# Attention and a mixture of experts in one kernel: attention order, routing, slot lists and slot tiles rewritten

## The chip, the cores and the metric

The kernel runs on one core of a Trainium2 chip. The metric is the device time of one execution in microseconds (us). The engines are named as in the profile: PE (TensorE, with PEld for its weight loads), DVE (VectorE), ACT (ScalarE), POOL (GpSimd) and SP (SyncE, which here only issues DMAs). Each engine takes its instructions strictly in the order in which they are queued; an instruction that waits holds up those behind it.

## The reference

Eight sequences of 448 tokens with 12 heads of 64 values go through attention with normalised queries and keys. The 3584 rows of 768 values that come out go through one dense block and one of eight experts, chosen by the largest logit.

```python
def _attn_ref(q, k, v, g_q, g_k):            # 8 x 12 x 448 x 64
    q_n, k_n = rmsnorm(q, g_q), rmsnorm(k, g_k)
    scores = scale * np.matmul(q_n, k_n.transpose(0, 1, 3, 2))
    ...                                       # softmax over the keys
    return np.matmul(attn, v)
x = attn_out.transpose(0, 2, 1, 3).reshape(3584, 768)
y_dense = np.maximum(x @ w1_dense, 0.0) @ w2_dense      # 768 -> 512 -> 768
expert_idx = np.argmax(x @ w_gate, axis=1)              # 8 experts
gate_w = softmax(x @ w_gate)[expert_idx]
y_moe[mask] = gate_w[mask, None] * (np.maximum(x[mask] @ w1[e], 0.0) @ w2[e])
return y_dense + y_moe
```

## The kernel before

*Attention.* Two heads side by side are a pair, and two pairs a group `g`; there are 24 groups, three to a sequence `b`. A token's row is split as position p and j = 0..6, so that seven consecutive tokens lie in one partition and a partition's load is one run of 1792 bytes. `period(g)` is one turn of a software pipeline, an order written out by hand over i = 0..6: it issues the scores of group g+1 (`scores`, four products of 64x64 tiles for each j, then ACT's exponential into one of 14 buffers), the value products of group g (`attend`, 64 rows each, a pair of them on the two halves of the array), the division (`divide`), the transposes of the group two before (`xtrans`, `xturned`), normalising and turning of q and k of group g+2 (`normalise`, `transposes`, `turned`), squares, sums and norms of group g+3 (`squares` on POOL, `sums` on DVE, `norms` on ACT), and the loads of group g+5 on SP. v comes through POOL's queue, cast to bf16 on the way. One pool of four PSUM banks (`wk`) serves transposes, value products, dense block, logits and ranks; the tile that `norms` writes its result to is the tile that `xtrans` fills next.

*Dense block and routing.* `dense` runs the first dense product for a chunk of 128 tokens as filler between attention steps, four chunks a sequence of which the last overlaps the one before by 64 rows. `logits`, `choose`, `gates`, `ranks` and `places` find for each token its expert, its gate and its slot: tiles of 128 slots are given to experts in the order in which they fill. `scatter` writes a record per token (its row, its dense hidden row, gate and number, 2592 bytes) to its slot in a table in HBM.

*Slot tiles.* `listing` orders the tiles that are full after six sequences, `experts` and `gaps` finish the list and mark empty slots. `turn(t)` reads a tile's number from the list (`tei`) into a register of SP, loads gates and numbers, and loads the 128 records with a DMA transpose. `gemm1(t)` multiplies by the expert's first matrix (chosen by a register of PE, six products of 512 columns), ACT applies the relu and the gate, `htrans(t)` turns the hidden rows (four transposes), and `gemm2(t)` sums dense and expert product in one PSUM tile, which DVE copies out and an indirect DMA of POOL writes to the output. `tiles` keeps four loads ahead. 32 tiles run always; three more stand behind a branch at the end.

Of the kernel before, what the change touches and what calls it, by code (L numbers as in the profile page):

```python
# [18 lines left out]
def kernel(  # L19
# [28 lines left out]
    De = D + 1  # L48
    scale = 1.0 / (D ** 0.5)
    PE, DVE, ACT, POOL, SP = (mybir.EngineType.PE, mybir.EngineType.DVE,  # L50
# [8 lines left out]
    nc.scalar.preload_act_table_set("natural_log_exp_and_others")  # L59
    make_identity(nc, ident)  # L60
    eps_t = const.tile([P, 1], F32)
    nc.vector.memset(eps_t, 1e-6)
    gq2 = const.tile([P, 1], F32)
    gk2 = const.tile([P, 1], F32)
    for hh in range(2):
        nc.scalar.dma_start(gq2[hh * D:(hh + 1) * D, :], g_q.unsqueeze(1))
        nc.scalar.dma_start(gk2[hh * D:(hh + 1) * D, :], g_k.unsqueeze(1))
    gqk = const.tile([P, 1], F32)
    nc.vector.tensor_mul(gqk, gq2, gk2)


    NTL = N // P + E - 1
    XH = Dm // 2
    GO = XH + F // 2
    RW = GO + 8
    OOB = 1.0e6
    RND = 1.5 * 2.0 ** 30
    tri = const.tile([P, P], BF16)
    ones = const.tile([P, P], BF16)
    prio = const.tile([P, E], F32)  # L80
    pid = const.tile([P, 1], F32)
    dbase = const.tile([P, 4], F32)
    inval = const.tile([P, 4], F32)
    onef = const.tile([P, E], F32)
    oh = const.tile([P, B, 4, E], BF16)
    cnts = [const.tile([P, E], F32, name=f"cnt{i}") for i in range(2)]
    tops = [const.tile([P, E], F32, name=f"top{i}") for i in range(2)]
    curs = [const.tile([P, E], F32, name=f"cur{i}") for i in range(2)]
    tsi = const.tile([P, B, E], F32)
    rall = const.tile([P, 12, RW], F32)  # L90
    rb = [rall[:, 4 * i:4 * i + 4] for i in (1, 2, 0)]
    emask = const.tile([P, E], F32)
    lane = const.tile([P, 2], F32)
    pid1 = const.tile([P, 1], F32)
    tcol = const.tile([P, 1], BF16)
    tdiag = const.tile([P, NTL], BF16)
    iot = const.tile([P, NTL], F32)
    onehot = const.tile([P, NTL], BF16)
    tei = const.tile([1, 3, NTL], I32)
    free = const.tile([P, E], F32)  # L100
    slot = [const.tile([P, 4], I32, name=f"slot{i}") for i in range(2)]
# [4 lines left out]
    LATE, WPACE = 4, 1.75  # L106
    rec = nc.dram_tensor("records", (NTL * P, RW), F32).ap()
    tail = const.tile([P, NTL, 2], I32)

    def constants():  # L110
        nc.vector.memset(ones, 1.0)
        nc.vector.memset(onef, 1.0)
        nc.vector.memset(cnts[0], 63.5)
        nc.vector.memset(tops[0], 0.0)
        nc.vector.memset(free, 0.0)
        nc.vector.memset(curs[0], 0.0)
        nc.vector.memset(inval, 0.0)
        nc.vector.memset(inval[:D, 3:4], OOB)
        nc.gpsimd.affine_select(tri, ones, pattern=[[1, P]], compare_op=ALU.is_gt, fill=0.0,
                                base=0, channel_multiplier=-1)  # L120
        kw = dict(allow_small_or_imprecise_dtypes=True)
        nc.gpsimd.iota(prio, pattern=[[-1, E]], base=E, channel_multiplier=0, **kw)
        nc.gpsimd.iota(pid, pattern=[[0, 1]], base=0, channel_multiplier=P, **kw)
# [5 lines left out]
        nc.gpsimd.iota(iot, pattern=[[1, NTL]], base=0, channel_multiplier=0, **kw)  # L129
        nc.gpsimd.iota(emask, pattern=[[-16, E]], base=0, channel_multiplier=1, **kw)  # L130
        nc.gpsimd.memset(rall[:, :, GO:], 0.0)
        nc.vector.tensor_scalar(pid1, pid, float(P), None, op0=ALU.add)
        nc.vector.tensor_scalar(tcol, pid, 1.0 / P, None, op0=ALU.mult)
        nc.vector.tensor_scalar(tdiag, ident[:, :NTL], pid, 1.0 / P, op0=ALU.mult, op1=ALU.mult)
        w8 = one.tile([P, E], F32)
        w9 = one.tile([P, E], F32)
        nc.vector.tensor_scalar(w8, emask, 0.0, None, op0=ALU.is_ge)
        nc.vector.scalar_tensor_tensor(w9, in0=emask, scalar=15.5, in1=w8, op0=ALU.is_lt,
                                       op1=ALU.mult)
        nc.vector.tensor_mul(w8, w9, emask)  # L140
        nc.vector.tensor_reduce(lane[:, :1], w8, AX.X, ALU.add)
        nc.vector.tensor_scalar(lane[:, 1:], lane[:, :1], 8.0, float(P), op0=ALU.mult,
                                op1=ALU.subtract)
        nc.vector.tensor_copy(emask, w9)
        nc.gpsimd.memset(tail, int(OOB))

    wjobs = [(wgb, moe_w_gate.rearrange("(ko p) e -> p ko e", p=P)),
             (wd1, moe_w1_dense.rearrange("(ko p) f -> p ko f", p=P)),
             (wd2, moe_w2_dense.rearrange("(fo p) d -> p fo d", p=P))]
    for e in range(E):  # L150
        wjobs.append((we[:, e, 0].rearrange("p (ko f) -> p ko f", f=F),
                      moe_w1[e].rearrange("(ko p) f -> p ko f", p=P)))
        wjobs.append((we[:, e, 1].rearrange("p (fo d) -> p fo d", d=Dm),
                      moe_w2[e].rearrange("(fo p) d -> p fo d", p=P)))

    one = ctx.enter_context(tc.tile_pool(name="m_one", bufs=1))
    with tc.tile_pool(name="a_ld", bufs=2) as ld, \
         tc.tile_pool(name="a_sb", bufs=2) as sb, \
         tc.tile_pool(name="a_sc", bufs=2, space=bass.MemoryType.PSUM) as scp, \
         tc.tile_pool(name="a_wk", bufs=4, space=bass.MemoryType.PSUM) as wkp:  # L160
        xin, sqs, ssqs, rs, xn, qkT, exs, xas, xTs, avs, trs, xps = [{} for _ in range(12)]
        vabs = [sb.tile([P, 2, J, D + 2], BF16, name=f"va{i}", tag=f"va{i}", bufs=1)
                for i in range(3)]

        NX = 2 * J
        lflat = we.rearrange("p e a f -> p (e a f)")[:, -LATE * KD * F:]
        lds = [lflat[:, i * 4 * S:(i + 1) * 4 * S].bitcast(F32).rearrange("p (h s) -> p h s", h=2)
               for i in range(6)]
        xflat = sb.tile([P, NX * 2 * S], BF16, name="exf", tag="exf", bufs=1)
        XW = (KD + FT) * P  # L170
        HX = J * 2 * S
        xro = [i * XW for i in range(4)] + [HX + 6 * Dm]
        xrb = [xflat[:, o:o + XW].rearrange("p (k s) -> p k s", s=P) for o in xro]
        ysb = [xflat[:, HX + i * 2 * Dm:HX + (i + 1) * 2 * Dm].bitcast(F32)
               .rearrange("p (a d) -> p a d", a=2) for i in range(3)]
        exr = [xflat[:, i * 2 * S:(i + 1) * 2 * S].rearrange("p (h s) -> p h s", h=2)
               for i in range(NX)]

        def setup():
            for a in vabs:  # L180
                nc.vector.memset(a[:, :, :, D:], 1.0)

        def heads(src, h0, n):

            return src.rearrange("b h s d -> (b h) s d")[h0:h0 + n].rearrange(
                "(i r) (p j) d -> (r p) i (j d)", r=2, j=J)

        def load(g):
            if g < NG:
                for n, (name, src) in enumerate((("q", q), ("k", k))):  # L190
                    xin[name, g] = lds[g % 3 * 2 + n]
                    nc.sync.dma_start(xin[name, g], heads(src, 4 * g, 4))

        def load_v(u):
            if 2 * u >= NG:
                return
            x = ld.tile([P, 4, J * D], BF16, tag="xv", name="xv")
            for n in ((0, 2), (2, 4)) if u == 0 else ((0, 4),):
                nc.gpsimd.dma_start(x[:, n[0]:n[1]],
                                    heads(v, 8 * u + 2 * n[0], 2 * (n[1] - n[0])))  # L200
            for i in range(2):
                xin["v", 2 * u + i] = x[:, 2 * i:2 * i + 2]

        def values(g):
            nc.gpsimd.tensor_copy(vabs[g % 3][:, :, :, :D],
                                  xin["v", g].rearrange("p h (j d) -> p h j d", d=D))

        def squares(g, name, scalar=False):
            for hh in range(2):
                sqs[name, g, hh] = sb.tile([P, J * D], F32, tag="sq", name="sq", bufs=3)  # L210
                x = xin[name, g][:, hh]
                if scalar:
                    nc.scalar.activation(sqs[name, g, hh], x, AF.Square)
                else:
                    nc.gpsimd.tensor_mul(sqs[name, g, hh], x, x)  # L215

        def sums(g, name, hh):
            if g not in ssqs:
                ssqs[g] = sb.tile([P, 2, 2, J], F32, tag="ssq", name="ssq")
            nc.vector.tensor_reduce(ssqs[g][:, "qk".index(name), hh],  # L220
                                    sqs[name, g, hh].rearrange("p (j d) -> p j d", d=D), AX.X,
                                    ALU.add)
# [141 lines left out]
        def places(b):  # L364
# [13 lines left out]
            def bc(x):  # L378
                return x.unsqueeze(1).to_broadcast([P, 4, E])
# [432 lines left out]
```

## Time and profile before

| | |
|---|---|
| Time, median of three runs | 431.74 us (427.64 to 434.82) |
| Profiled execution | 433.15 us, span 431.4 us |
| Busy: PE, DVE, ACT, POOL | 355.2, 248.9, 222.3, 239.2 us |
| Weight loads (PEld) | 212.8 us |
| Mean granted clock of PE | 0.931 |
| DMA moved | 74.74 MB; software queue 42.8%, hardware queue 32.8% of 16 engines |

Busy time is the share in which an engine works, over the whole span. Matmuls are pipelined and their ends are modelled, so the time from one start to the next tells what a product costs, not its listed length. In a row of waits the columns are: who waited, for whom, us in all, how often, and the longest. In a row of the timeline they are: start, length, engine, line, operation, tiles, count; in brackets the idle time before it and what ended it. The granted clock is the share of full speed that the PE clock was given in that stretch. DMA's share is the time that packets took, over 16 engines; overlapping packets both count, so it can pass 1.

### The profile page before, as it was taken

What the parts mean: (1) busy time and instruction counts of PE and PEld (TensorE: products, weight loads), DVE (VectorE), ACT (ScalarE), POOL (GpSimd) and SP (SyncE); (2) the same over time, 40 slices, a digit from 0 to 9 for tenths busy, and PEclk for the clock granted to TensorE, in tenths of its full rate; (3) what the DMA queues carried; (4) which work ended last, traced back from release to release, by engine and by line L of the source; (5) the groups of instructions that cost most, each with busy time, mean ns of one, the idle gap of its engine ahead of it and who ended that gap; (6) DMA issues with size and microseconds to landing.
All of it is one profiled execution on the core that took longest, in us unless ns stands there. A gap on an engine that the chain in (4) does not pass through costs nothing. (4 is left out here: it accounts for less than half of the span.)

```text
span 431.4 us, 13075 instructions
## 1 busy us (share of the span) xinstructions
PE 355.2 (82%) x5173; PEld 212.8 (49%) x5173; DVE 248.9 (58%) x712; ACT 222.3 (52%) x353; POOL 239.2 (55%) x281
## 2 busy tenths in 40 slices
PE   0463688896898977988988969879999999999991
PEld 0132356554465544555555545435555555555550
DVE  1749778987788978788888875361212222122220
ACT  3551787685586775685785766122233232332320
POOL 2186789789689798698798760325122221221221
PEclk9999988999698998798898986899999999999997
DMA  7559998499395879779685589769997787677400
GB/s 187 196 113 196 169 221 219 76 291 245 56 297 163 189 193 246 164 186 208 147 229 102 124 153 202 168 137 195 235 222 159 191 168 195 174 166 178 119 21 29
DMA packets 88812, 74.74 MB, mean 173 GB/s; under 512 B 55137, under 2 KB 85089, under 8 KB 88691
## 3 DMA queue, kind: packets, MB, share of 16 engines
q0 software_dynamic: 24288, 41.31, 42.8%
q1 hardware_dynamic: 64144, 32.58, 32.8%
q8 instruction: 43, 0.70, 0.7%
q14 instruction: 17, 0.14, 0.1%
q10 hardware_dynamic: 320, 0.00, 0.0%
HBM read 61.40 MB, written 26.22 MB: 203 GB/s over the span
## 5 line engine op out<-in xcount | busy, mean ns | idle before, releaser
L272 ACT ACTIVATE exf<-sc 128x896 bf16<-128x896 f32 x168 | 147.8, 918 | 59.9 <-PE sc L269 59.0
L215 POOL TENSOR_TENSOR sq<-we 128x448 f32<-128x448 f32 x88 | 80.8, 941 | 19.9 <-DVE ssq L220 19.6
L726 DVE COPY exf<-yp 128x768 f32<-128x768 f32 x32 | 30.7, 958 | 100.8 <-PE yp L720 95.5
L727 POOL DMA_INDIRECT out_dram<-exf,tail x32 | 31.4, 980 | 97.0 <-DVE exf L726 92.0
L269 PE MATMUL sc<-y 64*64 64x448 bf16 x672 | 70.7, 417 | 7.9 <-ACT exf L272 5.6
L287 PE MATMUL av<-va,exf 64*128 64x65 bf16 x2688 | 67.5, 201 | 6.5 <-issue 4.3
L287 PEld LDWEIGHTS <-exf 64*128 64x128 bf16 x2688 | 53.9, 100 | 29.7 <-issue 25.6
L220 DVE TENSOR_REDUCE ssq<-sq 128x7 f32<-128x448 f32 x96 | 55.9, 613 | 8.8 <-POOL sq L215 4.3
L517 PE MATMUL ff<-wd,xT 128*128 128x512 bf16 x192 | 53.7, 424 | 7.2 <-DVE rall L296 7.2
L239 POOL TENSOR_TENSOR y<-we,r 128x448 bf16<-128x448 f32 x46 | 42.4, 950 | 23.3 <-ACT r L233 23.2
L708 ACT COPY heT<-hp 128x512 bf16<-128x512 bf16 x32 | 18.8, 587 | 67.8 <-PE hp L706 67.8
L499 POOL DMA_INDIRECT records<-rall,slot x32 | 33.1, 1034 | 34.4 <-DVE xT L313 14.3
L696 PE MATMUL he<-we,exf 128*128 x192 | 47.9, 387 | 0.6 <-issue 0.6
L715 PE MATMUL yp<-wd,exf 128*128 128x384 bf16 x256 | 47.3, 328 | 0.0
L720 PE MATMUL yp<-we,heT 128*128 x256 | 46.8, 326 | 0.0
L247 PE MATMUL tr<-ident,y 128*128 128x128 bf16 x336 | 26.7, 237 | 22.5 <-DVE y L239 21.8
L296 DVE TENSOR_TENSOR rall<-av,inv 128x256 bf16<-128x256 f32 x96 | 40.8, 425 | 3.3
L269 PEld LDWEIGHTS <-y 64*64 64x64 bf16 x672 | 20.5, 108 | 32.7 <-issue 22.5
L247 PEld LDWEIGHTS <-y 128*128 128x128 bf16 x336 | 21.8, 107 | 28.9 <-DVE y L239 22.7
L701 ACT ACTIVATE hs<-he,tail 128x512 bf16<-128x512 f32 x32 | 22.0, 689 | 26.5 <-PE he L696 25.5
L715 PEld LDWEIGHTS <-exf 128*128 128x128 bf16 x256 | 25.2, 99 | 20.3 <-issue 0.9
L720 PEld LDWEIGHTS <-heT 128*128 128x128 bf16 x256 | 25.0, 98 | 16.6
(146 smaller groups left out, 352.1 us busy)
## 6 DMA issues: line engine op xcount, KB each, us to landing
we<-in_moe_w_dram POOLq DMA_DIRECT2D x16, 768.0 KB, 8.5
we<-in_q_dram SPq DMA_DIRECT2D x24, 448.0 KB
we<-in_k_dram SPq DMA_DIRECT2D x24, 448.0 KB
xv<-in_v_dram POOLq DMA_DIRECT2D x11, 448.0 KB, 5.1
wd<-in_moe_w_dense_dram POOLq DMA_DIRECT2D x2, 768.0 KB
records<-rall,slot POOLq DMA_INDIRECT x32, 5.0
tail<-records SPq DMA_DIRECT2D x32, 1.0 KB
exf<-records SPq DMA_TRANSPOSE x32
```

Source lines behind the costliest of these rows:

```text
L215: nc.gpsimd.tensor_mul(sqs[name, g, hh], x, x)
L220: nc.vector.tensor_reduce(ssqs[g][:, "qk".index(name), hh], sqs[name, g, hh].rearrange("p (j d) -> p j d", d=D), AX.X, ALU.add)
L239: eng.tensor_mul(y[:, :, hh], xin[name, g][:, hh].rearrange("p (j d) -> p j d", d=D), rs[name, g][:, hh].unsqueeze(2).to_broadcast([P, J, D]))
L247: nc.tensor.transpose(ps[:, j], xn[name, g][:, j].rearrange("p h d -> p (h d)"), ident)
L269: nc.tensor.matmul(ps[r * D:(r + 1) * D, hh, :S], kT[rows, r, j], qT[rows, r].rearrange("p j s -> p (j s)"), start=True, stop=True)
L272: nc.scalar.activation(x, ps[:, :, :S], AF.Exp, scale=scale)
L287: nc.tensor.matmul(avs[hh, r][:, m], exs[g, j][rows, hh, QC[m]:QC[m] + P], va[rows, hh, j, :De], start=(j == 0), stop=(j == J - 1))
L296: nc.vector.tensor_mul(xas[b][:, :, h * D:(h + 1) * D], avs[hh, r][:, :, :D], inv.to_broadcast([P, 4, D]))
L517: nc.tensor.matmul(ff[0], xTs[b][:, kk, QC[m]:QC[m] + P], wd1[:, kk], start=(kk == 0), stop=(kk == KD - 1))
L696: nc.tensor.matmul(he, xRs[t][:, kk], we[:, bass.ds(eregs[t], 1), 0, kk * F:(kk + 1) * F] .rearrange("p o f -> p (o f)"), start=(kk == 0), ...
L715: nc.tensor.matmul(yp[:, dd, :HD], xRs[t][:, KD + i], wd2[:, i, dd * HD:(dd + 1) * HD], start=(i == 0), stop=False)
L720: nc.tensor.matmul(yp[:, dd, :HD], heTs[t][:, i], we[:, bass.ds(eregs[t], 1), 1, i * Dm + dd * HD:i * Dm + (dd + 1) * HD] .rearrange("p o ...
```

## The change

Attention. A partition now holds three consecutive tokens for j = 0..2 and 4..6, and the last 64 tokens of two heads share j = 3. A key chunk (j other than 3) is then 128 keys of one head: its scores are two products of 64x128 tiles, and its value products use all 128 rows; `single` does j = 3 with 64 rows. k and v load in runs of 768 and 256 bytes, three transfers each on SP; v comes as float32, without a cast. There are 13 buffers for exponentials. PSUM is cut into four pools: scores, value products (`av`), dense and first expert product (`A`), and one bank `B` for norms and all transposes. The pipeline's order is a list of steps, `PLAN`, one string for each of a sequence's three periods:

```diff
-        def period(g):
-            b, gb = divmod(g, NB)
-            more = g + 2 < NG, g + 3 < NG
-            for i in range(J):
-                if g + 1 < NG:
-                    scores(g + 1, i)
...
+        PLAN = [x.split() for x in (
+            """r s w w nq kh Sq f r s o0 a00 tq Mq Tq kp Lq F r s a01 Sk Lk d0 F F r s w tx Tx F F
+               r s o1 a10 Mk tk Tk va Lv F r s a11 lg sd we nm r s w w d1 ch f f f""",
...
+        def attend(g, hh, ms):
+            av = avs[hh][:, :, :4 * De].rearrange("p r (m e) -> p r m e", e=De)
+            for m in ms:
+                for r in range(GP):
+                    for j in range(4 * r, 4 * r + 3):
+                        nc.tensor.matmul(av[:, r, m], exs[g, j][:, hh, QC[m]:QC[m] + P],
+                                         vabs[g % 3][:, vslot(hh, j), :De], start=False,
+                                         stop=(j == 4 * r + 2), skip_group_check=True)
```

Here `s` is scores and exponential, `o` and `a` value products, `d` division, `nq`, `kh`, `kp` normalising q on DVE and one half of k on DVE and one on POOL, `tq`, `tk`, `tx` transposes with `Tq`, `Tk`, `Tx` their copies, `Sq`, `Sk` squares and `Mq`, `Mk` their sums (now one operation for both head pairs), `nm` norms, `L` loads, `va` the copy of v, `f`, `F` one dense product, `r` relu, `sd` scatter, `we` weights; `w` is a product of zeros, issued in the first sequence only and 20 times before the first load is in (`warm`). Norms of q and k go to a tile of `B` that stays theirs until q's transposes are done.

Dense block and routing. The last 64 tokens of two sequences form one joint chunk, seven chunks for two sequences in place of eight. Each expert has a fixed region of 28 tiles in the table, so a slot is base + rank; ranks sum the counts of earlier sequences on PE, and `places` is one multiply and one sum:

```diff
-            nc.vector.tensor_add(c1, rk[:, 4], c0)
-            nc.vector.tensor_scalar(np_, c1, RND, RND, op0=ALU.add, op1=ALU.subtract)
...
+            nc.vector.tensor_mul(rro[:, :, :E], rk, oh[:, b])
...
+                nc.vector.tensor_reduce(slot[b % 2], rro, AX.X, ALU.add)
```

Slot tiles. Tiles 0 to 23 have fixed experts, three each, with expert 7 last; three more take experts with a fourth tile that is over half full; three are shared by two experts with 64 slots each. Tiles beyond these 30 run in a loop that stands behind a branch after tile 15. The lists come from `listing`, `listing2` and `listing3`, written in small steps between other work (`routine`). A fixed tile's first product is computed already turned, with the expert's matrix as the stationary operand:

```diff
-            he = wkp.tile([P, F], F32, tag="wk", name="he")
-            for kk in range(KD):
-                nc.tensor.matmul(he, xRs[t][:, kk],
-                                 we[:, bass.ds(eregs[t], 1), 0, kk * F:(kk + 1) * F]
...
+            if t < KS:
+                e = slot_of(t)[1]
+                he = wap.tile([P, FT, P], F32, tag="A", name="he")
+                for i in range(FT):
+                    for kk in range(KD):
+                        w = (we[:, e, 0, kk * F:(kk + 1) * F]
+                             .rearrange("p (g f a) -> p g a f", g=FT // 2, a=2))
+                        nc.tensor.matmul(he[:, i], w[:, i // 2, i % 2],
+                                         xRs[t][:, kk // 2, kk % 2],
+                                         start=(kk == 0), stop=(kk == KD - 1))
+                heTs[t] = sb.tile([P, FT, P], BF16, tag="Tq", name="heT")
+                nc.scalar.activation(heTs[t], he, AF.Relu)
+                return
```

Dense and expert product go to two PSUM tiles: ACT copies the first out, DVE adds the second times the gate. The last tile is added in two halves. `tiles` keeps eight loads ahead. The DMA transpose reads 256 half records of 640 values in place of 128 of 1280. Weights load in runs of two rows, and those of expert 7 during the first tiles. `final` replaces `tail_and_slots`:

```diff
+        with tc.manual_schedule(engines={PE, POOL, SP, DVE, ACT}):
+            first()
+            for g in range(NG - 1):
+                period(g)
+            final()                     # ends with tiles(0, SUR), SUR = 16
...
+        ntot = nc.values_load(lst["tot"], min_val=0, max_val=NS)
+        with tc.If(ntot > 0):
+            with tc.For_i(NO + 2 * NH, NTL, 1) as i:
...
+        with tc.manual_schedule(engines={PE, POOL, SP, DVE, ACT}):
+            tiles(SUR, LAST)
```

The prologue `first` loads the gains as rows through POOL's queue and turns them with a product on PE, and splits the first squares and normalisings into halves on ACT, DVE and POOL.

More of the change, by code (lines that the diff above doesn't have):

```diff
@@ L58 @@
     ident = const.tile([P, P], BF16)
[L59 to L60 removed]
+    gqk = const.tile([P, 1], F32)
     eps_t = const.tile([P, 1], F32)
[L62 to L68, printed above, removed]
@@ L90 @@
     rall = const.tile([P, 12, RW], F32)
     rb = [rall[:, 4 * i:4 * i + 4] for i in (1, 2, 0)]
[L92 to L101, printed above, removed]
+    halves = rall.bitcast(BF16).rearrange("p m (a c) -> p m a c", a=2)
@@ L127, in constants @@
         nc.gpsimd.iota(dbase[D:, 3:4], pattern=[[0, 1]], base=J - 1, channel_multiplier=J, **kw)
[L129 to L156, printed above, removed]
+        nc.gpsimd.affine_select(tri, ones, pattern=[[1, P]], compare_op=ALU.is_gt, fill=0.0,
+                                base=0, channel_multiplier=-1)
+        nc.gpsimd.memset(rall[:, :, GO:GO + 4], 0.0)
+        nc.gpsimd.memset(rall[:, :, RW - 4:], 0.0)
+        nc.gpsimd.memset(rall[:, 0, F // 2:GO], 0.0)
+        nc.gpsimd.memset(rall[:, 0, GO + 4:], 0.0)
+        nc.gpsimd.memset(rall[:, 0, GO + 1:GO + 2].bitcast(I32), int(OOB))
     with tc.tile_pool(name="a_ld", bufs=2) as ld, \
@@ new lines, in gap, with routine @@
+        def gap(j):
+            i = nc.gpsimd.indirect_dma_start(
+                out=rec, out_offset=bass.IndirectOffsetOnAxis(ap=lst["gix"][:, j:j + 1], axis=0),
+                in_=rall[:, 0], in_offset=None, bounds_check=E * N - 1, oob_is_err=False)
+            apart(i, rows, "only slots without a token")
+            apart(i, early, "these tiles are full")
+            rows.append(i)
+            holes.append(i)
+        jobs = []
+        def routine(n):
+            while jobs and n:
+                if next(jobs[0], "end") == "end":
+                    jobs.pop(0)
+                else:
+                    n -= 1
@@ L520, in dense, with fill @@
                 relus.append((b, m, ff[0]))
+        def fill(n):
+            for _ in range(n):
+                dense(wap)
         def relu():
@@ L768, in tail_and_slots @@
-            tiles(0, LAST)
-        run({PE, POOL, SP, DVE, ACT})
-        tot = one.tile([1, 1], I32)
-        nc.vector.tensor_copy(tot, tsi[:1, B - 1, E - 1:])
-        ntot = nc.values_load(tot, min_val=0, max_val=NTL * P)
-        with tc.If(ntot > LAST * P):
-            with tc.manual_schedule(engines={PE, POOL, SP, DVE, ACT}):
-                for t in range(LAST, NTL):
-                    turn(t)
-                gemm1(LAST)
-                htrans(LAST)
-                tiles(LAST, NTL)
+            av = avp.tile([P, 2, 512], F32, tag="av", name="lp")
@@ L785 @@
+        with tc.manual_schedule(engines={PE, POOL, SP, DVE, ACT}):
+            tiles(SUR, LAST)
 _INS = ['q', 'k', 'v', 'g_q', 'g_k', 'moe_w_gate', 'moe_w1_dense', 'moe_w2_dense', 'moe_w1', 'moe_w2']
```

1185 lines of the change are left out of this document (728 added, 457 removed).

## The prediction

> **What bounds the kernel now.** I read the page, then cut the span at its visible borders and asked for the busy time of every engine in each stretch: length, busy time (count) of PE, weight loads, DVE, ACT and POOL, granted clock, DMA share, GB/s.
>
> ```profile
> 25.31:72.33 47.02, 29.75 (x680) 20.18 (x680) 37.52 (x90) 28.98 (x45) 36.55 (x50) 0.95 0.98 177
> 72.33:195.22 122.89, 105.63 (x2172) 64.95 (x2168) 101.07 (x309) 87.65 (x140) 102.23 (x116) 0.92 0.80 192
> 195.22:266.00 70.78, 61.90 (x1226) 38.13 (x1223) 54.35 (x182) 47.54 (x73) 51.01 (x59) 0.84 0.79 164
> 266.00:289.70 23.70, 18.51 (x227) 10.20 (x225) 12.97 (x69) 6.56 (x12) 5.49 (x7) 0.93 0.70 153
> 289.70:421.80 132.10, 132.09 (x822) 75.53 (x821) 31.08 (x42) 39.44 (x62) 35.15 (x37) 0.99 0.72 169
> 421.80:431.40 9.60, 0.00 (x1) 0.00 (x0) 0.96 (x1) 0.00 (x0) 0.98 (x1) 0.73 0.08 31
> ```
>
> Up to 25.3 us is the prologue; 25.3 to 266 holds periods 0 to 22 of attention; then come the last values and routing, the slot tiles, and a tail. The second row holds 84 exponentials, seven to a period, so twelve periods of 10.24 us. The 23 periods take 240.7 us, 10.46 each. In the middle stretch four engines are between 71% and 86% busy and none is full; the waits say how they hold one another.
>
> ```profile
> ACT exf L272 <- PE sc L269: 25.4, 24, 2.7
> ...
> PE xt L306 <- ACT xt L233: 7.0, 4, 2.2
> ```
>
> ACT waits for scores 2.1 us a period; PE, in strict order, waits for the norms, which hold the PSUM tile of its transposes. PE's steps are in the timeline of one period at full clock:
>
> ```profile
> 154.82 0.62 PE L287 MATMUL av<-va,exf 64*128 64x65 bf16 x28
> 155.37 0.38 PE L269 MATMUL sc<-y 64*64 64x448 bf16 x4
> 155.68 0.96 PE L247 MATMUL tr<-ident,y 128*128 128x128 bf16 x14
> 156.57 0.38 PE L269 MATMUL sc<-y 64*64 64x448 bf16 x4
> ```
>
> From start to start: 28 value products take 0.55 us (pairs on the two row halves, 39 ns a pair), four score products 0.31, fourteen transposes 0.89. The tiles are another regime: PE is busy 132.09 of 132.10 us, and one tile is
>
> ```profile
> 353.14 1.46 PE L696 MATMUL he<-we,exf 128*128 x6
> 354.44 1.46 PE L715 MATMUL yp<-wd,exf 128*128 128x384 bf16 x8
> 355.74 1.46 PE L720 MATMUL yp<-we,heT 128*128 x8
> 357.04 0.39 PE L706 MATMUL hp<-ident,hs 128*128 128x128 bf16 x4
> 357.26 1.46 PE L696 MATMUL he<-we,exf 128*128 x6
> ```
>
> that is 1.30 + 1.30 + 1.30 + 0.22 = 4.12 us, without a gap.
>
> **The change, part by part.** *Prologue, 25.3 us now.* One wait of DVE is for the gain vectors:
>
> ```profile
> 10.58 0.51 DVE L69 TENSOR_TENSOR gqk<-gq,gk 128x1 f32<-128x1 f32 x1 [4.33 <-DMA gk<-in_g_k_dram]
> ```
>
> The sums of k stand behind it. The new code loads the gains as rows through POOL's queue and turns them on PE, off this path: 3.5 us. Warm-up products let the first transposes run at 0.89 rather than 2 us, and halves split over DVE and POOL take some tenths more; k's loads, in smaller pieces, give some back. I take 20 us; the bounds are 18 (every part pays) and 25.3.
>
> *One period.* PE: per query chunk, scores become two 64x128 products for four 64x64 ones; both fill the array's rows and stream 448 columns, so 0.31 stays. Value products become 8 pairs and 48 full-row ones in place of 56 pairs: at 39 ns each nothing changes. Whether a full-row product hides its weight load is not shown by this line, but by the logits:
>
> ```profile
> 280.48 0.81 PE L321 MATMUL lp<-wgb,xT 128*128 128x8 bf16 x24
> 281.15 2.75 PE L517 MATMUL ff<-wd,xT 128*128 128x512 bf16 x12
> 283.74 0.18 PE L360 MATMUL rk<-oh,tri 128*128 128x32 bf16 x1
> ...
> 288.89 0.18 PE L463 MATMUL er<-onehot,tbf 128*1 128x35 bf16 x1 [2.20 <-DVE tbf L426]
> ```
>
> 24 full loads and products in 0.67 us, 28 ns each, so it does. Joint last chunks make seven dense products a period of eight, 2.59/12 = 0.22 us saved. PE's steps go from 7 x 0.31 + 2.2 + 0.89 + 0.5 + 1.7 + 0.35 = 7.8 to 7.6 us; at the granted 0.92 that is 8.5 to 8.3. The other prices, over the twelve periods (count, busy us, mean ns):
>
> ```profile
> L272 ACT ACTIVATE exf<-sc 128x896 bf16<-128x896 f32 x84 | 73.9, 919 | 25.7 <-PE sc L269 25.4
> L215 POOL TENSOR_TENSOR sq<-we 128x448 f32<-128x448 f32 x48 | 44.0, 942 | 10.2 <-DVE ssq L220 10.1
> ...
> L220 DVE TENSOR_REDUCE ssq<-sq 128x7 f32<-128x448 f32 x48 | 28.2, 614 | 3.1 <-POOL sq L215 2.8
> ...
> L239 POOL TENSOR_TENSOR y<-we,r 128x448 bf16<-128x448 f32 x23 | 21.2, 951 | 6.5 <-ACT r L233 6.5
> L296 DVE TENSOR_TENSOR rall<-av,inv 128x256 bf16<-128x256 f32 x48 | 20.4, 425 | 1.7
> L499 POOL DMA_INDIRECT records<-rall,slot x16 | 16.8, 1049 | 3.8 <-ACT r L233 1.5 <-issue 1.3 <-ACT ln L227 0.5
> L239 DVE TENSOR_TENSOR y<-we,xt 128x448 bf16<-128x448 f32 x24 | 13.8, 618 | 2.6 <-issue 1.3 <-PE xt L306 0.9 <-ACT exf L272 0.4
> ```
>
> From the multiply of 256 elements to the sum of 448 DVE's time grows by 0.19 us, 1 ns an element beside 0.17 us fixed. Two sums of 896 for four of 448: 2.1 for 2.46 us. Two divisions of 512 for four of 256: 1.36 for 1.7, and two reciprocals fewer. Half of k's normalising moves from POOL (-0.95) to DVE (+0.62). Routing drops from some 26 small operations a batch to 11, a third of that per period: about -0.9. DVE goes from 101.07/12 = 8.4 to 7.1 us, POOL from 8.5 to about 7.2 with v's issue gone, ACT stays at 7.3. What matters more: norms get a PSUM tile apart from the transposes they used to block, so the 0.6 us of that row goes from the 1.7 (10.24 - 8.5) by which PE stalls now; of the other 1.1 I take half to go, since DVE and POOL have more slack (estimate; bounds none and all). By the engines the period is 8.3 us of PE and 0.6 of stalls, 8.9.
>
> DMA speaks against that. Queues of the middle stretch (packets, MB, share of 16 engines):
>
> ```profile
> q0 software_dynamic: 8880, 12.31, 52.1%
> q1 hardware_dynamic: 6528, 11.01, 26.6%
> ```
>
> and of the tiles, 300 to 400 us:
>
> ```profile
> q1 hardware_dynamic: 37360, 8.46, 54.6%
> ```
>
> The first is 24 loads of q or k: 1.36 us of all engines a load, 80 ns a packet of 1.69 KB; the last gives 23 ns a packet of 226 bytes. On that line a 768-byte packet costs 44 ns, and k or v, now 512 of these and 256 of 256 bytes, 1.77 us. v leaves the software queue, where its share by bytes was 1.2 us. Per period: 0.80 x 10.24 = 8.2, + 0.4 + 1.77 - 1.2 = 9.2 us of packet time. The first 47 us ran at a share of 0.98, so 9.4 us is what such a period asks for. Between 8.9 and 9.4 I take 9.2; bounds 8.2 (ACT's 7.3 and some waits) and 10.5 (nothing gained). 23 x 9.2 = 211.6.
>
> The Trainium skill ("DMA: Bandwidth & Descriptors", Why small descriptors are slow) charges about three cycles a packet beside one per 32 bytes. By it a 768-byte packet would cost 37 ns, estimated from the 80, and the period would ask for 0.8 us less; the 23 ns row lies above it, so the row decides.
>
> *Last values and routing, 23.7 us now.* The chain to the expert list (2.20 us wait above, before the second tile) goes: the first 24 tiles have constant experts, and their slots come from counts taken earlier. Two fewer dense chunks stand here (2.6 us), the placing chain has 2 operations for 17 (about 2.5). I take 17; bounds 14.5 (PE's work alone) and 24.
>
> *Tiles.* The reference's routing of these inputs gives 409, 528, 432, 430, 448, 366, 478, 493 tokens: 27 tiles over half full and five halves, which 30 tiles hold; the loop for a surplus does not run. A fixed tile swaps six products of 512 columns for 24 of 128. By the transposes' 0.22/4 = 55 ns these take 1.32 us, and the turn of 0.22 goes: 3.92. Three other tiles keep 4.12. Three shared tiles use pairs of 64 columns, 4.4 if paired like scores (6.9 if not). 24 x 3.92 + 12.4 + 13.2 - 1.3 (the first product, counted ahead) = 118.4. In the middle stands a branch at which every engine drains: 1.5 us, between 0.5 and 5, since no row here has one under load; half the clock at the start, seen now, 1. Sum 121.
>
> The Trainium skill ("Runtime: NRT & Kernel Launch", Instruction fetch mechanics) says that a taken branch outside the fetched pages stalls on a fetch. No row here shows one; it names no time, and the bound of 5 stands without it.
>
> *Tail, 9.6 us now.*
>
> ```profile
> 421.84 0.96 DVE L726 COPY exf<-yp 128x768 f32<-128x768 f32 x1 [1.87 <-PE yp L720]
> ```
>
> The last tile is now finished in halves, -0.5, and no branch follows: 8.9.
>
> Sum: 20 + 211.6 + 17 + 121 + 8.9 = 378.5 us of span. The profiled execution took 433.15 for its 431.4, 1.7 more: 380.2, so 380. That execution lies 1.4 us above the median of 431.74 and inside its 427.64 to 434.82.
>
> **The rivals.**
> *A, ACT sets the pace.* If DMA packets overlap more than I allow (shares here count queued packets) and the clock stays up, ACT's 7.3 us and an idle tenth give 8.2 a period: 380 - 23 = 357. For it: ACT's waits are all for PE. Against: PE alone asks for 8.3 at 0.92.
> *B, the clock and DMA give nothing.* If the share stays at 0.80 to 0.88 under load, 9.2/0.88 = 10.4; if PE idles more often and its clock falls to the 0.84 of the third row, 7.6/0.84 = 9.0 and most of the stalls of now, 1.4, make 10.4. Then 380 + 28 = 408, prologue, routing and tiles alone. For it: that third row.
> *C, slower: the load queue.* SP now issues seven transfers a period for two, each waiting for the one eight before it to land. With a landing time L a period cannot be shorter than 7/8 L. Up to L = 10.5 it hides; from 13.2 the kernel is slower than before (2.3 us a period eat the rest); at 14 the period is 12.25 and the time 450. For it: a DMA share near 1. Against: four of the seven are of 32 KB, and no engine waits for q or k in the middle stretch.
> *D, the change doesn't do what it says:* the surplus loop runs, or shared tiles do not pair, 6.9 for 4.4: 388. The counts above speak against the first.
>
> **How the numbers follow.** Forecast with D 0.50, A 0.17, B 0.23, C 0.10. The range takes A's 357 as its lower end, and goes at the upper end to B with 0.2 us more a period: 357 to 412; beside it the forecast's own, 370 to 392. Two per cent, 8.6 us, is about what a measurement of this kernel tells from no change. A and the forecast are faster whole; of B, 0.04 may land within 2%. Faster 0.86, same 0.04, slower 0.10.
>
> **What would show it.** Right: periods of 9.2 us between loads, a DMA share near 1 in the middle, no PE wait for norms, steps of 3.92 us in fixed tiles, under 3 us at the branch. Wrong: waits of DVE or POOL for q, k or v (C); a granted clock under 0.85 (B); weight loads that add to the 55 ns; a prologue above 23 us.

## Result and the profile after

The changed kernel took 373.24 us (median of four runs, 372.94 to 377.9) where the kernel before took 433.28 on the same chip: a ratio of 0.871, 95% interval 0.858 to 0.885. The forecast was 380. The total came out 1.8% below it, but four of its five terms were off by more than that, and the reason given for the largest was wrong. That the total is so near is in part luck: -16.4 and +9.5 us cancel. Executions of one kernel differ by some per cent here (the last variant's six spread from 355.5 to 380.6 us), so a stage read from one profile can be several us from that kernel's middle.

The stages of the changed kernel, in the columns of the prediction's first table:

```profile
20.08:52.57 32.49, 28.88 (x463) 18.34 (x468) 30.27 (x52) 28.88 (x48) 26.34 (x22) 1.00 0.95 253
52.57:161.26 108.69, 91.75 (x1408) 57.52 (x1430) 91.30 (x177) 88.95 (x141) 84.74 (x77) 0.98 0.95 252
161.26:218.30 57.04, 49.34 (x792) 31.38 (x803) 45.36 (x97) 47.19 (x72) 40.07 (x40) 1.00 0.97 230
218.30:237.81 19.51, 14.95 (x185) 9.10 (x187) 10.54 (x50) 4.79 (x10) 6.21 (x7) 0.91 0.86 158
237.81:365.80 127.99, 123.31 (x1132) 85.17 (x1133) 37.53 (x87) 45.58 (x67) 41.41 (x45) 0.97 0.89 180
365.80:371.70 5.90, 0.02 (x1) 0.00 (x0) 0.62 (x1) 0.00 (x0) 0.98 (x1) 0.69 0.09 36
```

The second row holds twelve periods of 9.06 us; ACT is busy 7.4 us of each, PE 7.65, DVE 7.6, POOL 7.1, at a clock of 0.98 where it was 0.92. Against the sum of the prediction:

| stage | before | predicted | measured | off by |
|---|---|---|---|---|
| prologue | 25.3 | 20 | 20.1 | +0.1 |
| 23 periods | 240.7 | 211.6 (9.2 each) | 198.2 (8.62 each) | -13.4 |
| last values and routing | 23.7 | 17 | 19.5 | +2.5 |
| tiles | 132.1 | 121 | 128.0 | +7.0 |
| tail | 9.6 | 8.9 | 5.9 | -3.0 |

Waits of the middle stretch:

```profile
ACT exf L339 <- PE sc L337: 15.4, 25, 2.0
...
DVE inv L369 <- PE sc L337: 9.0, 5, 1.9
...
PE tq L313 <- DVE xn L300: 5.4, 11, 0.7
...
POOL xn L297 <- DMA we<-in_k_dram: 5.0, 3, 3.0
```

No wait of PE for the norms is left. But a mean period hides most of this kernel. Cut from one group's first score product to the next's, the periods of a sequence are of three kinds. One sequence of the kernel before:

```profile
97.33:112.55 15.22, 10.14 (x201) 5.99 (x200) 12.30 (x43) 8.15 (x15) 12.67 (x16) 0.88 0.77 182
112.55:122.50 9.95, 9.95 (x175) 5.62 (x175) 7.23 (x21) 7.05 (x10) 6.84 (x8) 0.85 0.74 148
122.50:130.03 7.53, 7.38 (x169) 4.67 (x169) 5.92 (x15) 6.56 (x11) 7.23 (x9) 1.00 1.05 300
```

and one of the changed kernel:

```profile
92.98:103.52 10.54, 8.37 (x135) 5.34 (x138) 7.29 (x12) 7.77 (x13) 7.90 (x8) 1.00 0.90 278
103.52:113.02 9.50, 7.72 (x116) 4.65 (x118) 9.06 (x21) 7.45 (x13) 7.95 (x7) 1.00 0.99 242
113.02:120.62 7.60, 7.18 (x108) 4.39 (x108) 6.58 (x14) 6.92 (x11) 5.52 (x6) 1.00 1.05 261
```

The period without routing, called light below, takes 7.53 us before and 7.60 after: full-row value products, joined operations and the norms' own place together did not shorten it. The long one, 13.9 us in the mean of five sequences, now takes 10.3; the second 9.0 for 9.6. The start is the other part: period 0 took 18.3 us and takes 8.1, since PE used to stand behind constants that DVE made there (27.43 to 37.77 us):

```profile
31.71 4.62 DVE L138 SCALAR_TENSOR_TENSOR w<-emask,w 128x8 f32<-128x8 f32 x1
32.40 1.83 POOL L239 TENSOR_TENSOR y<-we,r 128x448 bf16<-128x448 f32 x2
34.20 1.81 POOL L215 TENSOR_TENSOR sq<-we 128x448 f32<-128x448 f32 x2
36.37 0.17 DVE L140 TENSOR_TENSOR w<-w,emask 128x8 f32<-128x8 f32 x1
...
38.88 1.68 PE L247 MATMUL tr<-ident,y 128*128 128x128 bf16 x14 [7.87 <-DVE y L239]
```

Nearly half of that is one operation on eight columns. It lasted 4.62 us, until four large operations of POOL were done; its neighbour of the same size took 0.17. The experiment on the norms below shows the same picture.

### The profile page after: what moved, and what is told of

Same layout as the page of the kernel before. It is cut to its first block, busy times and chain, and to the rows that moved or that the text cites. A ratio compares the mean times of both kernels' runs of the same rounds, so it can differ in the third digit from the quotient of the medians.

```text
span 371.7 us, 10446 instructions
## 1 busy us (share of the span) xinstructions
PE 323.5 (87%) x4056; PEld 207.6 (56%) x4102; DVE 228.1 (61%) x488; ACT 226.9 (61%) x355; POOL 213.4 (57%) x222
## 5 line engine op out<-in xcount | busy, mean ns | idle before, releaser
L257 POOL TENSOR_TENSOR sq<-we 128x896 f32<-128x896 f32 (+1 forms) x43 | 72.4, 1683 | 2.1 <-DMA we<-in_k_dram 1.9
L337 PE MATMUL sc<-T 64*128 64x448 bf16 (+1 forms) x384 | 61.7, 363 | 12.4 <-ACT exf L339 8.8
L262 DVE TENSOR_REDUCE ssq<-sq 128x14 f32<-128x896 f32 (+1 forms) x48 | 49.6, 1039 | 6.6 <-ACT sq L255 4.0
L361 PE MATMUL av<-va,exf 128*128 128x66 bf16 x1152 | 52.9, 195 | 0.0
L1008 PE MATMUL yp<-we,heT 128*128 128x384 bf16 (+3 forms) x264 | 44.4, 328 | 0.8 <-DVE rall L1014 0.8
L966 PEld LDWEIGHTS <-we 128*128 128x128 bf16 x576 | 36.1, 99 | 8.1 <-issue 4.3
L371 DVE TENSOR_TENSOR rall<-av,inv 128x512 bf16<-128x512 f32 x48 | 33.2, 691 | 1.7
L1008 PEld LDWEIGHTS <-heT 128*128 128x128 bf16 (+1 forms) x264 | 23.9, 100 | 17.0 <-issue 2.5
L297 POOL TENSOR_TENSOR xn<-we,r 128x448 bf16<-128x448 f32 x25 | 23.9, 958 | 15.2 <-DMA we<-in_k_dram 7.4
L303 DVE TENSOR_TENSOR xn<-we,tq 128x896 bf16<-128x896 f32 x23 | 24.8, 1080 | 1.4 <-POOL rall L257 0.8
```

The source lines that it names most:

```text
L257: nc.gpsimd.tensor_mul(y, x, x)
L262: nc.vector.tensor_reduce(ssqs[g][:, "qk".index(name), hs], sqs[name, g].rearrange("p (h j d) -> p h j d", h=2, d=D)[:, hs], AX.X, ALU.add)
L337: nc.tensor.matmul(ps[o, hh, :S], kT[rows, j * P + o.start:j * P + o.stop], qT[rows, r * S:(r + 1) * S], start=True, stop=True)
L361: nc.tensor.matmul(av[:, r, m], exs[g, j][:, hh, QC[m]:QC[m] + P], vabs[g % 3][:, vslot(hh, j), :De], start=False, stop=(j == 4 * r + 2), ...
L371: nc.vector.tensor_mul(xas[b].rearrange("p m a c -> p (m a) c")[:, :, o:o + D] .rearrange("p n (r d) -> p r n d", r=2), av[:, :, :, :Dh], ...
L966: nc.tensor.matmul(he[:, i], w[:, i // 2, i % 2], xRs[t][:, kk // 2, kk % 2], start=(kk == 0), stop=(kk == KD - 1))
```

## Experiments

**The start: the clock, or the work?** First zero products added to the kernel before:

```diff
+            for _ in range(2 if g == 0 else 1 if g < 4 else 0):
+                nc.tensor.matmul(ps[:, 0], zrow[:, :P], zrow, start=True, stop=True)
...
+                for _ in range(20):
+                    nc.tensor.matmul(un[:, 0], zrow[:, :P], zrow, start=True, stop=True)
                 load(0)
```

> The kernel before, with products of zeros added: 20 before the first load is in, two ahead of each score step of group 0 and one ahead of each of groups 1 to 3, into the bank that the scores then overwrite. Theory (clock): the start of the kernel before ran at half clock, so prologue and first periods lose 5 to 10 us by this alone, 422 to 428 us. Rival (loads): the first 47 us ran at a DMA share of 0.98 and at stalls on loads and constants, the clock did not decide, and the time stays within 2 us of before.

Measured: 431.27 us, 1.011 times before (1.004 to 1.017): a little slower, by less than 2%. The zero products did raise the clock: between 17.6 and 30.4 us four score products took 0.38 us where they had taken 0.59. But period 0 took 20.0 us for 18.3, for PE then waited 7.98 us for DVE as it had waited 7.87, and went on at half clock (fourteen transposes 1.68 us for 0.95). Then the changed kernel without its zero products (`warm` issues none), twice, the second time beside the changed kernel itself:

> The changed kernel without its products of zeros (before the first load and in the first sequence). Theory (clock): the five first periods took 6.7 us because PE was at full clock; without the products prologue and first periods are longer by 6 to 12 us, 379 to 385 us. Rival: the first periods are short because they hold no dense products, no scatters and few weights; then only the prologue loses 1 to 2 us, 374 to 375 us.

> The changed kernel without its products of zeros, again, beside the changed kernel on one chip. If the products are worth their place (clock theory), 2 us or more slower than the changed kernel. If they only stand in PE's order ahead of work that could start, which the first run of this variant suggests (prologue and first five periods 56.5 us against 52.6, but the whole not slower), equal within 3 us or a few us faster.

> The changed kernel itself, beside the variants of this call on the same chip. Expected 365 to 378 us. If the 3.35 us wait of PE ahead of the fifth tile's first product, behind a wait of ACT for no instruction that the trace shows, belongs to the program, it stands at the same place again; if it comes from what the DMA queues happen to do, it stands elsewhere or not at all, and the span is some 6 us shorter or longer by that alone.

Measured: without them 363.66 us on one chip (0.839 of before, 0.830 to 0.849) and 371.90 on another (0.869, 0.860 to 0.877), where the changed kernel took 372.97 (0.868, 0.859 to 0.877). So they are worth nothing that shows: in the second pair periods 0 to 4 took 40.2 us without them and 38.9 with them, and the whole is equal. (Cut at score products, the first five periods take 7.8 us each in the changed kernel, not the 6.7 of the expectation.) No run shows a gain of the whole from the clock; what went from period 0 is the wait for constants.

**DMA.** The changed kernel without most of v's loads:

```diff
+                if name == "v" and g > 1:
+                    xin[name, g] = xin[name, g - 2]
+                    continue
```

> The changed kernel without v's loads from group 2 on (it reuses the values of groups 0 and 1, so 22 of 24 groups get wrong values): three transfers and some 1.7 us of packet time fewer a period, nothing else. Theory (DMA sets the middle periods, 8.6 us of packet time in 9.06): a period falls to the next bound, ACT and PE with their waits, 8.0 to 8.5 us, and the whole by 12 to 22 us, 351 to 361 us. Rival (the engines' chain sets the period and DMA is only nearly full): within 4 us of the changed kernel, 369 to 374 us.

The wrong values route the tokens otherwise, so that the loop for surplus tiles runs and the whole takes 907.92 us; only the attention can be read. Its twelve periods from group 6's scores to group 18's:

```profile
58.90:160.80 101.90, 94.77 (x1435) 57.81 (x1434) 91.20 (x178) 88.08 (x141) 85.49 (x76) 0.98 0.83 217
```

8.49 us each. That looked like the theory until the last experiment below, which loads v whole, showed the same stretch:

```profile
59.20:161.10 101.90, 93.68 (x1435) 56.84 (x1434) 91.15 (x178) 87.91 (x141) 85.38 (x76) 1.00 1.00 269
```

The same 101.90 us at a DMA share of 0.83 and of 1.00. v's loads do not set the period; a share of 1 is no bound here.

**Which operations count.** Norms apart, in the kernel before (a spare buffer of `lo` was given up for room):

```diff
-            trs["x"] = wkp.tile([P, 1024], BF16, tag="wk", name="xt")
-            rs["q", g] = trs["x"][:, GP * S:].bitcast(F32)[:, :2 * J].rearrange(
-                "p (h j) -> p h j", h=2)
+            rs["q", g] = sb.tile([P, 2, J], F32, tag="rq", name="rq")
...
```

> The kernel before, with the norms of q and k written to a tile of SBUF instead of the PSUM bank that the next transposes of attention rows take; the transposes then allocate a bank only when they start. Nothing else changes. My theory credits this part with 0.6 us of each of 23 periods: some 14 us less, about 418 us, and the row 'PE xt <- ACT xt' of the waits gone. Rival: the wait only moves (PE waits for the next exponential or bank in its place) and the time stays within 3 us of before.

Measured: 459.07 us, 1.070 times before (1.060 to 1.079), which neither side expected. The group of DVE's normalising (count, busy us, mean ns) and two of them in the timeline:

```profile
L237 DVE TENSOR_TENSOR y<-we,rq 128x448 bf16<-128x448 f32 x48 | 72.7, 1555 | 4.5 <-ACT rq L231 4.4
```

```profile
163.24 5.63 DVE L237 TENSOR_TENSOR y<-we,rq 128x448 bf16<-128x448 f32 x2
164.01 1.86 POOL L237 TENSOR_TENSOR y<-we,r 128x448 bf16<-128x448 f32 x2
165.80 1.83 POOL L215 TENSOR_TENSOR sq<-we 128x448 f32<-128x448 f32 x2
```

The same operation took 618 ns with its norms in PSUM. With both inputs in SBUF, two of them lasted 5.63 us beside four of POOL's; the six of this line that had no operation of POOL beside them took 0.61 to 0.63 us. The Trainium skill ("SBUF — State Buffer", Who interferes with whom) says that a VectorE instruction with two SBUF inputs contends with a GpSimd instruction that reads SBUF; these rows agree. So the experiment moved two things, and whether the shared bank cost 0.6 us a period stays open; what it showed is a reason to keep q's norms in PSUM, as both kernels do.

DVE's and POOL's joined operations cut in two again, in the changed kernel:

```diff
-                    sums(g + 3, x)
+                    for hh in range(2):
+                        sums(g + 3, x, slice(hh, hh + 1))
...
+            for r in range(2):
+                nc.vector.reciprocal(inv[:, r], av[:, r, :, Dh:])
```

> The changed kernel with DVE's and POOL's joined operations cut in two again: squares and sums by head pair (448 elements), reciprocals and divisions by half (256 elements). By the durations DVE works 0.30 + 0.51 = 0.81 us more a period (7.6 to 8.4), POOL 0.35 more. My prediction's step: half of the slack that these operations free becomes time, so some 0.4 us a period, 9 us in all, back again. Rival: neither engine sets the period (DMA and the chain of PE and ACT do), 0 to 3 us.

Measured: 374.33 us, 0.870 of before (0.862 to 0.877), beside 0.868. The light periods rose from 7.6 to 8.1 us, about as far as the prediction's step would have it, so these operations do count there. In the medians of the whole 1.4 us is left of it, inside the rival's 0 to 3. But each interval spans some 3 us either way, and in the two profiles, from one chip, the 23 periods took 203.6 us here and 198.4 in the changed kernel, so the total does not settle it.

**Where routing stands.** In the kernel before, its second half was moved one period on:

```diff
+                    if gb == 2 and g > 2:
+                        ranks(b - 1)
+                        gates(b - 1)
+                        places(b - 1)
                     send()
...
-                    if gb == 1 and g > 1:
-                        ranks(b - 1)
```

> The kernel before, with ranks, gates and places of a sequence moved from the end of the period that also holds its logits and choice to the step before the scatters of the next period. No operation is added or left out. What the traces showed by now: without routing a period takes 7.5 us in the kernel before and 7.6 in the changed one; the period with the whole routing took 13.9 in the mean of five, 10.3 in the changed kernel, which spreads it over three. New theory: the gain of the middle comes from where routing's chain stands; then the long period falls by 2 to 3 us, the next one rises by up to 1, and the whole by 8 to 20 us, 410 to 421 at 430 before. Rival (the number of DVE operations counts, not their place): within 3 us of before.

Measured: 442.81 us, 1.030 times before (1.023 to 1.038). Slower, so my new theory failed in this form. The period that the chain left fell from 13.9 to 10.8 us, a little more than forecast, but the one that it entered rose from 9.6 to 13.9, where at most 1 us was forecast. The waits say why:

```profile
PEld L517 <- DVE free L401: 22.7, 7, 3.7
```

Dense products wait for the last of `places`' 18 operations, 3.2 us in each of seven sequences: the chain works in a PSUM bank of the pool that the dense block takes its banks from. Where it stands, the period is long.

In the changed kernel all routing was put into one period again:

```diff
-  ... sd we nm r s w w d1 ch f f f
+  ... sd we nm r s w w d1 ch eg oh rk pl ga f f f
```

> The changed kernel with all of a sequence's routing in the first of its three periods: logits, choice, gates' exponential, totals, ranks, places and gates one after the other at its end, as before the change they stood in one period. New theory: that period rises from 10.3 us by 2 to 3, the second one falls by 0.5 to 1, and the whole rises by 8 to 17 us, 378 to 388 at 370. Rival (place does not matter, only the number of operations): within 3 us of the changed kernel.

Measured: 385.93 us, 0.892 of before (0.886 to 0.897), 11 us more than the variant with moved DMAs below, which ran on the same chip. The period with routing takes 11.7 us for 10.3 in the mean of five. A sequence of three periods takes 31.1 us before, 28.3 in this variant, 26.9 in the changed kernel: by these profiles spreading is worth 1.4 of the 4.2. That share is loose: in other profiles with the changed kernel's attention code a sequence takes 25.5 (the last experiment) to 27.6 us (the variant with moved DMAs). Most of the gain is there with the routing in one place. The chain is short in it and its scratch lies in spare columns of the value products' bank; which of the two counts was not tried apart.

**Tiles.** The fixed tiles' first product in the old form (`gemm1` takes the path of six products of 512 columns, `htrans` turns the result):

> The changed kernel with the first product of its 24 fixed tiles in the old form: six products of 512 columns with the constant expert, relu, four transposes and a copy. From the trace 1.30 + 0.22 = 1.52 us for 1.39: 24 x 0.13 = 3 us slower than the changed kernel, 4.12 us a tile for 3.98. Rival: the old form's extra turn through ACT adds waits of PE for the hidden rows, 6 us or more.

Measured: 370.95 us, 0.865 of before (0.857 to 0.874), beside 0.868: no slower. A tile does take 4.12 us, as this timeline shows from one first product to the next,

```profile
272.88 1.46 PE L980 MATMUL he<-we,xr 128*128 128x512 bf16 x6
...
277.00 0.81 PE L980 MATMUL he<-we,xr 128*128 128x512 bf16 x3
```

where the changed kernel takes 3.98:

```profile
263.82 1.55 PE L966 MATMUL he<-exf,we 128*128 128x128 bf16 x24
265.21 1.46 PE L999 MATMUL yd<-wd,exf 128*128 128x384 bf16 x8
266.51 1.46 PE L1008 MATMUL yp<-we,heT 128*128 128x384 bf16 x8
267.81 1.55 PE L966 MATMUL he<-exf,we 128*128 128x128 bf16 x24
```

but the 3.4 us that this variant loses so (24 x 0.14) it gains at the one stall early in the tiles, which is 1.34 us in it, with no half clock behind it. In the changed kernel:

```profile
247.56 0.98 POOL L658 DMA_INDIRECT records<-rall,gix  x1 [0.30 <-issue]
248.84 0.98 POOL L1017 DMA_INDIRECT out_dram<-exf,tail  x1 [0.30 <-issue]
250.12 0.98 POOL L658 DMA_INDIRECT records<-rall,gix  x1 [0.30 <-issue]
...
252.60 0.60 ACT L970 ACTIVATE heT<-he 128x512 bf16<-128x512 f32 x1 [7.14 <-remote]
...
253.24 2.72 PE L966 MATMUL he<-exf,we 128*128 128x128 bf16 x24 [3.35 <-ACT heT L970]
```

ACT's relu needs a product that PE ended at about 247.3, and starts at 252.60; PE then waits 3.35 us for it, and works at half clock behind it (granted clock 0.50 from 253.24 to 258.32): this group and the next take 5.08 us from start to start for the usual 2.69. The trace names no instruction that ACT waited for ("remote"). The run of the changed kernel again had it at the same place (3.20 us). POOL had been issuing indirect DMAs one after the other, among them those that mark empty slots. These were moved:

```diff
-                for j in [range(3), [3], [4], [5], [6], [7]][t] if t < 6 else []:
+                for j in {3: range(3), 4: range(3, 5), 5: range(5, 8)}.get(t, []):
```

> The changed kernel with the eight DMAs that mark empty slots issued three in tile 3, two in tile 4 and three in tile 5, where they stood three in tile 0 and one in each of tiles 1 to 5. Theory (these DMAs hold up what runs beside them): the wait of PE of 3.3 us ahead of the fifth tile's first product, with two half-clock groups behind it, goes or moves behind tile 4. Rival (they have no part in it): it stands at the same place, 3.2 to 3.5 us, and tiles take 125 to 126 us from the first dense product to the last as before.

Measured: 375.01 us, 0.871 of before (0.864 to 0.879). The stall moved three tiles on, and again ended behind POOL's row, 4.33 us long for PE:

```profile
264.90 0.98 POOL L658 DMA_INDIRECT records<-rall,gix  x1 [0.30 <-issue]
...
267.46 0.60 ACT L970 ACTIVATE heT<-he 128x512 bf16<-128x512 f32 x1 [8.14 <-remote]
```

Last, the same DMAs spread:

```diff
+                for j in [[0], [1], [2], [3], [4, 5], [6, 7]][t] if t < 6 else []:
```

> The changed kernel with the same eight DMAs for empty slots, one behind each of tiles 0 to 3 and two behind tiles 4 and 5, so that POOL never issues more than three indirect DMAs in a row (the output's among them). What the traces showed: in six runs POOL issued five or more in a row beside the tiles, ACT's relu stood still meanwhile, and it went on 1.3 to 1.6 us after the last of them had been issued; with the DMAs moved by three tiles the wait moved by three tiles. Theory (a row of them is what holds the engines up): no wait of PE over 1 us between the first tile and the branch, tiles 119.5 to 121 us from the first dense product to the last for 125 to 126, and the whole some 5.5 us less than the changed kernel, 364 to 368 us. Rival (their number counts, not the row): the wait stands elsewhere in the same size, 370 to 374 us.

Measured: six runs fell apart into 355.5 and 356.6 and four from 364.8 to 380.6, median 366.6, beside 428.78 for before; no interval could be given, so that it is faster than the changed kernel is not shown. In the profiled run (span 354.9) ACT's long wait is gone, and PE's longest in the tiles is another one:

```profile
274.81 1.56 PE L966 MATMUL he<-exf,we 128*128 128x128 bf16 x24 [2.47 <-DMA exf<-records]
```

Tiles took 122.9 us from the first dense product to the last, for 126.3 in the first profile and 125.1 in the second, above the 119.5 to 121 expected. Of the 16.8 us by which its span is shorter than the first profile's 371.7, only some 3.4 lie in the tiles; the 23 periods, whose code is the same, take 188.9 us for 198.2.

## Why the prediction was right and wrong

*Prologue.* 20 predicted, 20.1 measured. The share that the zero products were given in it does not show as such: on one chip the prologue took 20.2 with them and 20.4 without.

*The period, 9.2.* The number was near the middle's 9.06; the reason was wrong. The step that failed is the one from DMA packets to the period: "0.80 x 10.24 = 8.2, + 0.4 + 1.77 - 1.2 = 9.2 us of packet time" was taken for what the period must last. Packet time came to 0.95 x 9.06 = 8.6 us. The price of a load was not what missed: without v's loads the hardware queue's share of the 8.49 us falls from 0.545 to 0.356, so a load of v took 1.6 us for my 1.77. The software queue fell by more than I took off, from 0.521 x 10.24 = 5.3 us to 0.424 x 9.06 = 3.8. The Trainium skill's rule ("DMA: Bandwidth & Descriptors", Why small descriptors are slow) had put the whole at 8.4, by the prediction's estimate, with some 1.4 us for that load; the 1.6 measured lies between the rule and my line, a little nearer to the line. But the stretch lasts 101.9 us with and without v's loads, so packet time was not its bound. Rival A named the mechanism: packets overlap, the clock stays up (0.98), and the engines set the pace. In the last experiment's profile the 23 periods take 188.9 us, 8.21 each, which is A's 8.2. That ACT is the engine which sets it is not shown: in that profile's twelve periods ACT is busy 7.3 us of 8.49 and PE 7.8. C fell: there was its sign, POOL waiting for k three times in twelve periods, but only 5.0 us in all.

The rest of the miss, 8.62 for 9.2 over all periods, lies at the ends: periods 0 to 4 took 38.8 us (7.8 each), where 46 were forecast. They hold little dense work and routing, and the 10.2 us that period 0 lost to constants were in none of my steps. I had averaged twelve periods of three kinds, and so priced operations where, as far as the runs go, the long period's chain was the cost: the routing's operations, worth 0.9 us of DVE in my sum, stood on the path of one period in three.

*The edits costed at nothing.* Full-row products: the light period of 7.60 beside 7.53 does not tell, since the joined operations alone move it by 0.5 us. That part alone was not tried, and stays open.

*Last values and routing.* 17 predicted, 19.5 in the first profile, 17.0 in that of the changed kernel's second run and 15.2 in the last experiment's. In the first, one wait is of the kind met in the tiles. Here POOL's two scatters are the row, PE's last value product ends near 223.3, and DVE starts 2.6 us later:

```profile
222.37 0.93 PE L361 MATMUL av<-va,exf 128*128 128x66 bf16 x24
...
222.70 1.06 POOL L677 DMA_INDIRECT records<-rall,slot  x1 [10.94 <-DVE xT L395]
...
224.06 0.97 POOL L677 DMA_INDIRECT records<-rall,slot  x1 [0.30 <-issue]
225.88 0.26 DVE L369 RECIPROCAL inv<-av 128x16 f32<-128x16 f32 x1 [3.58 <-remote]
```

In the profile of the last experiment DVE starts in the middle of the same two scatters, 0.03 us after the products are done:

```profile
213.32 0.93 PE L361 MATMUL av<-va,exf 128*128 128x66 bf16 x24
213.64 1.06 POOL L677 DMA_INDIRECT records<-rall,slot  x1 [10.05 <-DVE xT L395]
...
214.28 0.26 DVE L369 RECIPROCAL inv<-av 128x16 f32<-128x16 f32 x1 [1.03 <-PE av L361]
...
215.00 0.97 POOL L677 DMA_INDIRECT records<-rall,slot  x1 [0.30 <-issue]
```

The placing chain that went had 18 operations, not 17.

*Tiles.* 121 predicted, 128.0 measured. The stall with the half clock behind it is 3.35 + (5.08 - 2.69) = 5.7 us, and in none of my steps; 24 products of 128 columns take 1.39 us and not 1.32, another 1.7. The branch was oversized, 0.6 us where 1.5 was taken:

```profile
306.33 1.46 PE L1008 MATMUL yp<-we,heT 128*128 128x384 bf16 x8
308.25 1.55 PE L966 MATMUL he<-exf,we 128*128 128x128 bf16 x24 [0.45 <-PEq L1108]
```

From start to start 1.92 us for the usual 1.30. On the fetch that the Trainium skill ("Runtime: NRT & Kernel Launch", Instruction fetch mechanics) warns of, these rows show no more than this. D fell too: no surplus tile ran, and the shared tiles, 4.36 and 4.57 us from one first product to the next, do pair.

*Tail.* 5.9 for 8.9. The last store is issued at 367.25 and the span ends 4.4 us later, where before it took 8.3 from that issue (423.07 to 431.4), with the branch behind it. I had taken off only 0.2 for that; that the branch is what cost the rest was not tried by itself.

## What to carry to other kernels

Cut a software pipeline by what each period holds before you average: the period without the rare work tells what the edits did to the core, and here that was 0.07 us in all, while the periods with routing and the start paid for the change. A DMA share near 1 need not be a bound, as twelve periods of 101.90 us at 0.83 and at 1.00 show; take a load away before calling it one. A chain of small operations costs what waits for it and for its PSUM bank, so look for what waits there before moving it.

## What was not expected of the hardware

In some executions ACT and DVE went on only after POOL had issued a row of indirect DMAs, though PE's product was long done. In six profiles with six or more in a row beside the tiles, ACT started 1.3 to 1.6 us after the last one's issue had ended, and the trace named nothing that it waited for; with the old tile form it also started 1.5 us after it, but there the trace names a product of PE. In other executions, the last experiment's among them, scatters held nobody up. The periods with scatters show it too: 10.3 us in the first profile and 9.1 in the last one's mean of five, so part of the spread from 355 to 381 us may be this. That the wait moved when the DMAs were moved is shown; why it comes in one execution and not in another, and whether it is the row, is open. The first run without zero products kept the row of six and had no such wait, but PE waited 5.2 us there a little later for a tile's record load, so a tile can lose as much in another way.
